# Softmax denominators: ones-products on TensorE against 32x32 transposes and sums on VectorE

## Chip, cores and metric

The kernel runs on one core of one Trainium2 chip, in float32 throughout. The metric is the device time of one execution in microseconds (us), as the median of repeated runs. The engines are TensorE (PE in the profile; its weight loads are listed apart as PEld), VectorE (DVE), ScalarE (ACT), GpSimd (POOL) and the queue that issues the transfers (SP).

## What is computed

Attention over 8 sequences, 12 heads, 448 tokens and 64 values a head, with q and k normalised by their root mean square, followed by a gated feed-forward block of width 1536 on the 3584 rows of 768. Cut to what matters here:

```
q_n, k_n = rmsnorm(q, g_q), rmsnorm(k, g_k)
scores = q_n @ k_n.T / sqrt(64)
attn = exp(scores - max)
attn = attn / (sum(attn, axis=-1) + 1e-9)     # the denominators
x = attn @ v                                  # then (B,H,S,D) -> (B*S, H*D)
xn = x / rms(x) * rms_g
out = (silu(xn @ w_gate) * (xn @ w_val)) @ w_out
```

## The kernel before

The function that runs is `safe_scores`; a second function, `any_scores`, follows only where a flag computed from g_q and g_k asks for it, which it does not for these inputs. The exponentials are taken without the maximum, which a bound on the scores allows.

**Pairs and blocks.** Work goes by pairs of heads: 48 pairs g, six to a sequence (NPAIR = 6). Scores lie transposed, keys on partitions and the 448 queries along the columns, so that a denominator is a sum over partitions. From pair 7 on, a block of the program does seven times: scores of pair g for 64 keys of both heads (`scores`, L659), the weighted values of pair g-1 (`weighted`, L674), and the exponentials (`exps`, ScalarE, L664) into a tile e. These matmuls use quarters of the array (64 by 64). After the block come feed-forward steps (`todo`, run by `fill`), and the turning of the next pair's q and k (`turn`).

**The order.** It is written out by hand: each engine gets its instructions in the order in which the program issues them. The program counts steps: every call of `pe(fn)` is one step, which runs `fn` and then whatever `after(n, ...)` has put down for that step. A block takes four steps for its scores and values, then about 9 to 17 for the rest. In the first sequence's feed-forward steps the weights are also converted (`convert`, with `join` on VectorE, L917 to L919), one piece after most steps. For the second and third sequences VectorE also makes combinations of weights (L1091, L1094, L1126, L1154 to L1157).

**The denominators.** `later_sums(g, 2)`, called at the end of the block's four steps, has GpSimd add the seven tiles e of pair g into a tile es (L709, L714) over the next steps: the first add two steps later, the last ones three steps after that. In es, 64 partitions belong to each head. `totals(g)` runs for g = 7 alone, and then for two pairs at a time, (8, 9), (10, 11) up to (46, 47), in the first step of the block after the second pair, ahead of that block's scores. For each pair and head a matmul with a 64x64 matrix of ones (L692) gives the sum over the 64 partitions, repeated on 64 rows, in a bank `den` of the pool `ps_s` (four banks, shared with the scores). ScalarE copies den into a tile rd (L696, and L699 in two halves). `invert` (L595 to L599) then has VectorE transpose rd in 32x32 blocks, take the reciprocal of one column of each block (14 columns), and transpose these columns, broadcast, back into rd. `weigh` (L638) multiplies the values by rd: for the older pair at once, from a copy in SBUF that `hold` made; for the newer in the block's last step, from PSUM.

Each float32 matmul stands in the trace as two passes, so its rows count double.

Of the kernel before, what the change touches and what calls it, by code (L numbers as in the profile page):

```python
# [22 lines left out]
NPAIR = H // 2  # L23
# [312 lines left out]
def safe_scores(  # L336
# [62 lines left out]
    def own(j):  # L399
        return slice(j * D, (j + 1) * D)  # L400

    def across(j):
        return own(1 - j)
# [189 lines left out]
    def invert(rd, den):  # L593

        few = tmp.tile([128, S // 32], F32, name="few", tag="few", bufs=1)  # L595
        squares_of = lambda t: t.rearrange("p (n c) -> p n c", c=32)
        nc.vector.transpose(out=squares_of(rd), in_=squares_of(den))
        nc.vector.reciprocal(few, squares_of(rd)[:, :, 0])
        nc.vector.transpose(out=squares_of(rd), in_=few.unsqueeze(2).to_broadcast([128, S // 32, 32]))  # L599
# [22 lines left out]
    def close(g):  # L622
        for key in [key for key in st if key[0] == "e" and key[1] == g]:
            st.pop(key)
        for key in ("qk", "v", "qT", "kT", "rs", "ms"):
            st.pop((key, g))

    def hold(g):

        nc.scalar.copy(x_of(g), st.pop(("av", g))[:, 0:S])  # L630
        close(g)
# [45 lines left out]
    def step(g, i):  # L677
# [3 lines left out]
        if ps is not None:  # L681
            exps(g, i, ps)

    def totals(g):

        which = (g, g - 1) if g > NPAIR + 1 else (g,)
        den = {i: ps_s.tile([128, 512], F32, name="den", tag="s") for i in which[::-1]}
        for i in which:
            es = st.pop(("es", i))
            for j in range(2):  # L690
                to = j if i == g else 1 - j
                nc.tensor.matmul(den[i][own(to), 0:S], lhsT=ones[across(j)], rhs=es[across(j)], start=True, stop=True)  # L692
        for i in which[::-1]:
            rd = st["rd", i] = tmp.tile([128, S], F32, name="rd", tag="rd", bufs=2)
            if i == g:
                nc.scalar.copy(rd, den[i][:, 0:S])  # L696
            else:
                for j in range(2):
                    nc.scalar.copy(rd[own(j)], den[i][across(j), 0:S])  # L699
        for i in which[::-1]:  # L700
            invert(st["rd", i], st["rd", i])
            if i < g:
                weigh(i, 3, 4)

    def later_sums(g, n):

        def first():
            st["es", g] = tmp.tile([128, S], F32, name="es", tag="es", bufs=2)
            nc.gpsimd.tensor_tensor(st["es", g], st["e", g, 0], st["e", g, 1], ALU.add)  # L709
            more(2)  # L710

        def more(*parts):
            for i in parts:
                nc.gpsimd.tensor_tensor(st["es", g], st["es", g], st["e", g, i], ALU.add)  # L714

        after(n, first)
        after(n + 2, lambda: more(3, 4))
        after(n + 3, lambda: more(5, 6))


    def rms_x(b):
# [1022 lines left out]
    load_v(1)  # L1744
    gqk = const.tile([128, 1], F32, name="gqk")
    rg = const.tile([128, NDC], F32, name="rg")
    row = const.tile([1, 2, D], F32, name="row")

    def gains():


        nc.vector.scalar_tensor_tensor(gqk, gq, D**0.5, gk, ALU.mult, ALU.mult)
        nc.vector.tensor_scalar(gqk, gqk, SAFE, -SAFE, ALU.min, ALU.max)
# [51 lines left out]
    for g in range(NG + 1):  # L1805
        b, hp = divmod(g, NPAIR)
        if g:
            load_pair(g + 3)
        if hp == 2:
            for i in range(2):  # L1810
                load_rests(b + 1, i, nc.sync)
            load_v_rests(b + 1)
        if g == 0:
            pe(lambda: score(0, (0,)))
            pe(lambda: rests(0))
            pe(lambda: score(0, (1,)))
            pe(lambda: turn(1, 0))
            pe(lambda: score(0, (2,)))
            norm_rests(0, 2, 4)
            squares(2, 0)  # L1820
            squares(2, 1)
            pe(lambda: turn(1, 1))
            for _ in range(3):
                convert()
            load_pair(3)
            load_v(2)
            convert()
            load_rows()
            continue
        if g <= NPAIR:  # L1830
            pe(lambda: score(g, (0,)))
            squares(g + 2, 0)
            squares(g + 2, 1)
            if g > 1:
                pe(lambda: turn(g + 1, 0))
                some_rests(g)
                pe(lambda: turn(g + 1, 1))
            pe(lambda: rests(g))
            pe(lambda: values(g - 1))
            if g == 1:  # L1840
                pe(lambda: turn(g + 1, 0))
                some_rests(g)
                pe(lambda: turn(g + 1, 1))
            load_v(g + 2)

            turns(1 if g == 1 else 3 if g < NPAIR else 0)
            pe(lambda: sums(g - 1))
            pe(lambda: score(g, (1, 2)))
            turns(2 if g == 1 else 3 if g == NPAIR else 0)
            if g == 2:  # L1850
                bound()
            if g == NPAIR - 1:
                for half in range(2):
                    norm_k(g + 2, half)
            continue

        if g == NPAIR + 1:
            some = lambda *parts: [exps(g, i, scores(g, i)) for i in parts]
            pe(lambda: (rests(g), some(0, 1)))
            pe(lambda: values(g - 1))  # L1860
            pe(lambda: rms_x(0))
            pe(lambda: some(2, 3))
            pe(lambda: some(4, 5))
            pe(lambda: norm_x(0))
            pe(lambda: sums(g - 1))
            later_sums(g, 2)
            begin(0, 15)
        else:
            sums_due = g % 2 == 0
            pe(lambda: (totals(g - 1) if sums_due else None, step(g, 0)))  # L1870
            if st.pop("held", None):
                convert()
            pe(lambda: [step(g, i) for i in (1, 2)])
            pe(lambda: [step(g, i) for i in (3, 4)])
            pe(lambda: ([step(g, i) for i in (5, 6)], weigh(g - 1, 2) if sums_due else hold(g - 1)))
            if g < NG:
                later_sums(g, 2)
        st["block"] = now["t"]
        after(2, lambda g=g: load_v(g + 2))
        if hp:  # L1880
            fill()
            norm_k(g + 1, 0)
            squares(g + 2, 0)
            squares(g + 2, 1)
            pe(lambda: turn(g + 1, 0))
            norm_k(g + 1, 1)
            some_rests(g)
            fill()
            pe(lambda: turn(g + 1, 1))
            fill(hold=g % 2 == 1)  # L1890
            continue
        fill(3)
        norm_k(g + 1, 0)
        fill(2)
        pe(lambda: turn(g + 1, 0))
        norm_k(g + 1, 1)
        fill(1)
        pe(lambda: rms_x(b - 1))
        squares(g + 2, 0)
        squares(g + 2, 1)  # L1900
        pe(lambda: turn(g + 1, 1))
        fill(len(todo))
        begin(b - 1, 16)
        pe(lambda: norm_x(b - 1))
        fill()
# [41 lines left out]
```

## Time and profile before

| what | value |
|---|---|
| median of 3 runs | 1515.41 us (1513.07 to 1515.65) |
| profiled execution, span | 1514.0 us |
| PE busy | 1478.8 us (98%) |
| PEld busy | 1154.0 us (76%) |
| DVE busy | 1037.7 us (69%) |
| ACT busy | 602.2 us (40%) |
| POOL busy | 741.3 us (49%) |
| products of the denominators (L692) | 164 rows, 113.2 to 1292.0 us |

The page gives the profiled execution by its span, from the first instruction to the last; what lies around the span is not in it. A share of busy time is a mean over stretches that differ: the first 110 us are attention alone, to about 250 us the weights are converted beside the first feed-forward block, and the rest repeats by sequences. In a timeline row stand the start, the length, engine, line, operation, written tile and read tiles, shapes and count; in brackets the idle time before it and what ended it. In a row of groups stand the count, then busy time, mean ns of one, and the idle time before them.

### The profile page before, as it was taken

The page shows a single profiled execution, that of the slowest core. Times are in us where ns is not written, and L with a number is a line of the kernel's source. Part 1 is how long each engine was busy: PE and PEld are TensorE (multiplying, and loading weights), DVE is VectorE, ACT ScalarE, POOL GpSimd, SP SyncE. Part 2 cuts the span into 40 slices and gives each one's busy share as a digit, 9 for nine tenths or more (in the row PEclk, how much of TensorE's full clock was granted, in tenths as well). Part 3 has the DMA queues.
Part 4 walks back from the last instruction along what each step waited for, and adds up shares of the span by engine and source line. Part 5 has one row for each costly group of instructions (what it writes and reads, how often), then busy time and mean ns, then how long its engine had stood idle before and what let it go on. Part 6 is the DMA issues. An engine that isn't in the chain of part 4 may idle for free.

```text
span 1514.0 us, 25709 instructions
## 1 busy us (share of the span) xinstructions
PE 1478.8 (98%) x8732; PEld 1154.0 (76%) x8732; DVE 1037.7 (69%) x1826; ACT 602.2 (40%) x1377; POOL 741.3 (49%) x708
## 2 busy tenths in 40 slices
PE   8999999999899999999999999999999999999997
PEld 4344445678755888878888888768888789899997
DVE  5788999699944697874568555535668655684664
ACT  6856764344323433234343443443542433101100
POOL 6867997556423454564535643445645731021002
PEclk9999999999999999999999999999999999999999
DMA  7758675776667899996558855585558655587675
GB/s 200 227 159 252 174 247 174 228 249 206 224 219 224 266 316 312 301 291 180 163 150 257 244 176 153 165 255 159 153 153 255 216 162 139 165 292 234 174 228 180
DMA packets 302176, 322.51 MB, mean 213 GB/s; under 512 B 81620, under 2 KB 243668, under 8 KB 302036
## 3 DMA queue, kind: packets, MB, share of 16 engines
q1 hardware_dynamic: 301108, 320.58, 69.4%
q8 instruction: 72, 1.18, 0.3%
q14 instruction: 68, 0.56, 0.1%
q10 hardware_dynamic: 800, 0.20, 0.1%
q0 software_dynamic: 128, 0.00, 0.0%
HBM read 266.90 MB, written 53.77 MB: 212 GB/s over the span
## 4 chain that ended last, share of the span: by engine, by line
PE 84%; DVE 8%; DMA 3%; issue 1%; SPq 1%; POOL 1%; ACT 0%; DVEq 0%; POOLq 0%
PE ff L1191 37%; PE ff L1532 13%; PE sc L659 7%; PE av L674 7%; PE ff L1604 6%; PE ff L1461 5%; PE tr L545 2%; PE den L692 1%; PE den L607 1%; PE sc L563 1%; PE av L590 1%; PE ff L1334 1%; DVE l L1406 1%; DMA w<-kept 1%; DVE w L1091 1%
## 5 line engine op out<-in xcount | busy, mean ns | idle before, releaser
L1191 PE MATMUL ff<-x,w 128*128 128x224 f32 x1296 | 259.6, 353 | 1.4 <-DVE pb L1212 1.1
L714 POOL TENSOR_TENSOR es<-es,e 128x448 f32<-128x448 f32 x205 | 253.4, 1236 | 13.6
L1191 PEld LDWEIGHTS ff<-x,w 128*128 128x128 f32 x1296 | 242.7, 190 | 5.4 <-DVE pb L1212 1.4
L659 PE MATMUL sc<-qT,kT 64*64 64x448 f32 x1176 | 231.0, 539 | 0.7 <-DVE x L744 0.7
L674 PE MATMUL av<-e,vt 64*64 64x448 f32 x984 | 193.1, 538 | 0.0
L664 ACT ACTIVATE e<-sc 128x448 f32<-128x448 f32 x294 | 154.2, 547 | 72.6 <-PE sc L659 57.1
L1191 PE MATMUL ff<-xs,w 128*128 128x224 f32 x832 | 165.0, 353 | 2.9 <-issue 1.6
L1191 PEld LDWEIGHTS ff<-xs,w 128*128 128x128 f32 x832 | 155.7, 190 | 6.2 <-issue 3.0
L644 POOL TENSOR_TENSOR ss<-ss,rd 128x448 f32<-128x448 f32 x40 | 47.1, 1178 | 207.2 <-ACT rd L643 206.5
L709 POOL TENSOR_TENSOR es<-e 128x448 f32<-128x448 f32 x41 | 49.2, 1200 | 192.3 <-ACT e L664 192.3
L659 PEld LDWEIGHTS sc<-qT,kT 64*64 64x64 f32 x1176 | 79.2, 133 | 82.1 <-issue 60.1
L1532 PE MATMUL ff<-w,l 128*128 128x192 f32 x630 | 117.8, 328 | 3.7 <-DVE pa L1567 1.7
L515 POOL TENSOR_TENSOR rs<-ms,mhalf 128x12 f32<-128x12 f32 (+1 forms) x50 | 115.9, 2319 | 4.2
L1212 DVE TENSOR_TENSOR pc<-ff,l 128x448 f32<-128x448 f32 x56 | 34.8, 622 | 115.7 <-PE ff L1191 80.9
L1604 PE MATMUL ff<-x,w 128*128 128x448 f32 x288 | 111.8, 541 | 0.0
L1532 PEld LDWEIGHTS ff<-w,l 128*128 128x128 f32 x630 | 103.8, 190 | 8.7 <-DVE pa L1567 2.9
L674 PEld LDWEIGHTS av<-e,vt 64*64 64x64 f32 x984 | 66.0, 133 | 41.6 <-issue 41.6
L1604 PEld LDWEIGHTS ff<-x,w 128*128 128x128 f32 x288 | 53.3, 190 | 51.1 <-issue 48.2
L1191 PE MATMUL ff<-top_x,w 128*128 128x224 f32 x440 | 91.1, 356 | 0.0
L1209 DVE TENSOR_TENSOR pb<-ff,pb 128x448 f32<-128x448 f32 x84 | 52.3, 623 | 56.1 <-PE ff L1191 50.3
L1191 PEld LDWEIGHTS ff<-top_x,w 128*128 128x128 f32 x440 | 81.8, 190 | 11.3 <-issue 8.5
L1191 PE MATMUL ff<-l,w 128*128 128x224 f32 x416 | 83.6, 353 | 1.1 <-DVE pc L1212 1.1
(212 smaller groups left out, 2806.1 us busy)
## 6 DMA issues: line engine op xcount, KB each, us to landing
w<-kept SPq DMA_DIRECT2D x380, 256.0 KB, 3.5
w<-kept_q SPq DMA_DIRECT2D x350, 192.0 KB, 3.8
w<-kept_o SPq DMA_DIRECT2D x150, 192.0 KB, 3.6
kept_q<-w SPq DMA_DIRECT2D x63, 192.0 KB, 3.9
qk<-in_q_dram SPq DMA_DIRECT2D x48, 192.0 KB, 3.7
qk<-in_k_dram SPq DMA_DIRECT2D x96, 96.0 KB, 3.7
raw<-in_moe_w_gate_dram SPq DMA_DIRECT2D x24, 384.0 KB, 4.8
raw<-in_moe_w_val_dram SPq DMA_DIRECT2D x24, 384.0 KB, 4.4
```

The costliest lines, as they stand in the source:

```text
L515: nc.gpsimd.tensor_tensor(st["rs", g][:, cols], ms, mhalf[:, cols], ALU.pow)
L644: after(m, lambda: (nc.gpsimd.tensor_tensor(ss, ss, rd, ALU.add), st.update({("summed", b): hp})))
L659: nc.tensor.matmul(ps[r, 0:S], lhsT=st["kT", g][r, keys_of(i)], rhs=st["qT", g][r, :], start=True, stop=True)
L664: nc.scalar.activation(e, ps[:, 0:S], ACT.Exp)
L674: nc.tensor.matmul(st["av", g][own(j), 0:S], lhsT=vt, rhs=st["e", g, i][r], start=i == 0, stop=i == PARTS - 1, skip_group_check=True)
L709: nc.gpsimd.tensor_tensor(st["es", g], st["e", g, 0], st["e", g, 1], ALU.add)
L714: nc.gpsimd.tensor_tensor(st["es", g], st["es", g], st["e", g, i], ALU.add)
L1191: nc.tensor.matmul(bank[:, w * HT:(w + 1) * HT], lhsT=data(key)[:, (2 * w + c) * 128:(2 * w + c + 1) * 128], rhs=a[left][:, c, :], start=o ...
L1209: nc.vector.tensor_tensor(T[name], ps[:, 0:S], T[name], ALU.add)
L1461: nc.tensor.matmul(ps, lhsT=left_o(b, which, LEFT_O[name], c), rhs=data(("wo", b, name, c)), start=first and c == 0, stop=c == NFP - 1, sk ...
L1532: nc.tensor.matmul(ps, lhsT=a[:, j, :], rhs=data(key)[:, n % 2 * HW:(n % 2 + 1) * HW], start=start and j == 0, stop=j == KG - 1, skip_grou ...
L1604: nc.tensor.matmul(bank[w][:, 0:S], lhsT=data(key)[:, c * 128:(c + 1) * 128], rhs=st["x", 0][:, 3 * half + c, :], start=half == c == 0, st ...
```

## The change

The sum over partitions is split. A new function `fold(g)` has VectorE transpose es in 32x32 blocks in place and sum each block's rows to one column: 14 columns for a pair, in which each of the four quarters of 32 partitions holds its own part of the sums. It is put down for eight steps after the first add of es, or is run by `totals` itself if that comes first. `totals` then has one matmul with a constant 128x128 matrix `other` of zeros and ones, which adds the two quarters of each head, for both pairs together (28 columns). VectorE takes the reciprocal of the 28 columns from PSUM, and transposes 14 of them, broadcast, into each pair's rd. The ones-products, ScalarE's copies into rd and `invert`'s first transposes go from `totals` (`invert` stays for the first pairs, in `sums`). The matrix `other` is made once, by four sums over parts of the identity matrix, at pair 2. The tile `row` of the flag's computation moves from a pool of constants to a buffer of the output tiles' pool.

```
+    def fold(g):
+        es = blocks(st.pop(("es", g)))
+        nc.vector.transpose(out=es, in_=es)
+        if "few_d" not in st:
+            st["few_d"] = tmp.tile([128, 2, S // 32], F32, name="few_d", tag="few_d", bufs=1)
+        nc.vector.tensor_reduce(out=st["few_d"][:, g % 2], in_=es, axis=AX_X, op=ALU.add)

     def totals(g):
-        which = (g, g - 1) if g > NPAIR + 1 else (g,)
-        den = {i: ps_s.tile([128, 512], F32, name="den", tag="s") for i in which[::-1]}
+        which = (g - 1, g) if g > NPAIR + 1 else (g,)
         for i in which:
-            es = st.pop(("es", i))
-            for j in range(2):
-                to = j if i == g else 1 - j
-                nc.tensor.matmul(den[i][own(to), 0:S], lhsT=ones[across(j)], rhs=es[across(j)], start=True, stop=True)
-        for i in which[::-1]:
+            if ("es", i) in st:
+                fold(i)
+        few, n = st.pop("few_d"), len(which)
+        den = ps_s.tile([128, 512], F32, name="den", tag="s")[:, 0:n * S // 32]
+        nc.tensor.matmul(den, lhsT=other, rhs=few[:, 2 - n:].rearrange("p i n -> p (i n)"), start=True, stop=True)
+        few = tmp.tile([128, 2, S // 32], F32, name="few_r", tag="few_r", bufs=1)[:, 2 - n:]
+        nc.vector.reciprocal(few.rearrange("p i n -> p (i n)"), den)
+        for at, i in enumerate(which):
             rd = st["rd", i] = tmp.tile([128, S], F32, name="rd", tag="rd", bufs=2)
-            if i == g:
-                nc.scalar.copy(rd, den[i][:, 0:S])
-            else:
-                for j in range(2):
-                    nc.scalar.copy(rd[own(j)], den[i][across(j), 0:S])
-        for i in which[::-1]:
-            invert(st["rd", i], st["rd", i])
+            nc.vector.transpose(out=blocks(rd), in_=few[:, at].unsqueeze(2).to_broadcast([128, S // 32, 32]))
             if i < g:
                 weigh(i, 3, 4)
...
         after(n + 3, lambda: more(5, 6))
+        after(n + 8, lambda: fold(g) if ("es", g) in st else None)
...
-    row = const.tile([1, 2, D], F32, name="row")
+    row = y_pool.tile([1, 2, D], F32, name="y", tag="y")
+    other = const.tile([128, 128], F32, name="other")
+    def one_per_quarter():
+        for j in range(2):
+            for n in range(2):
+                cols = slice(j * D + n * 32, j * D + n * 32 + 32)
+                nc.vector.tensor_reduce(out=other[:, cols], in_=ident[:, across(j)].rearrange("p (n c) -> p c n", c=32),
+                                        axis=AX_X, op=ALU.add)
...
             if g == 2:
                 bound()
+                one_per_quarter()
```

More of the change, by code (lines that the diff above doesn't have):

```diff
@@ L626, in close, with blocks @@
             st.pop((key, g))
+    def blocks(t):
+        return t.rearrange("p (n c) -> p n c", c=32)
     def hold(g):
```

## The prediction

> **What bounds the kernel now.** I read the page first (span, busy shares, the forty slices, the chain that ended last), then busy times by stage, then the timelines around the denominators.
>
> ```profile
> span 1514.0 us, 25709 instructions
> ...
> PE 1478.8 (98%) x8732; PEld 1154.0 (76%) x8732; DVE 1037.7 (69%) x1826; ACT 602.2 (40%) x1377; POOL 741.3 (49%) x708
> ...
> DVE  5788999699944697874568555535668655684664
> ...
> PE 84%; DVE 8%; DMA 3%; issue 1%; SPq 1%; POOL 1%; ACT 0%; DVEq 0%; POOLq 0%
> ```
>
> TensorE (PE) carries 84% of the chain, VectorE (DVE) 8%. But DVE's digits are 9 in slices 4 to 11 (37.9 us each), so the share of 69% hides a stretch where DVE is full:
>
> ```profile
> 113.00:208.00 95.00, 95.00 (x449) 45.29 (x452) 84.34 (x125) 63.97 (x151) 84.10 (x77) 1.00 0.75 218
> 208.00:250.00 42.00, 41.31 (x195) 20.84 (x199) 40.93 (x63) 24.86 (x57) 34.01 (x31) 1.00 0.71 210
> 290.00:330.00 40.00, 37.85 (x229) 33.02 (x227) 38.30 (x60) 13.69 (x31) 20.33 (x20) 1.00 0.74 242
> 386.00:416.00 30.00, 26.41 (x171) 20.38 (x168) 27.95 (x45) 11.75 (x27) 15.44 (x13) 1.00 0.59 190
> 416.00:457.00 41.00, 38.57 (x157) 21.20 (x157) 17.05 (x37) 9.51 (x23) 10.75 (x10) 0.96 0.72 224
> 457.00:1290.00 833.00, 826.41 (x5261) 690.29 (x5261) 531.56 (x943) 328.52 (x761) 403.04 (x379) 1.00 0.70 213
> ```
>
> The columns are the stretch, its length, busy time of PE, weight load, DVE, ACT, POOL, then clock and DMA. To 208 us PE never rests and DVE is 89% busy; to 250 DVE is 97% busy; at 290 to 330 and 386 to 416 DVE is over 93% busy while PE loses 2.2 and 3.6 us; after 457 PE loses 6.6 us in 833 and DVE is 64% busy. So the change must be priced in three stretches.
>
> **What the old denominators cost PE.** Every second pair's block carries the products; the other is the same block without them.
>
> ```profile
> 860.08 0.59 PE L659 MATMUL sc<-qT,kT 64*64 64x448 f32 x2
> 865.50 0.84 PE L1191 MATMUL ff<-top_x,w 128*128 128x224 f32 x3
> 889.17 0.98 PE L692 MATMUL den<-es,ones 64*64 64x448 f32 x8
> 895.34 0.83 PE L1191 MATMUL ff<-top_x,w 128*128 128x224 f32 x3
> 401.65 0.86 PE L726 MATMUL msx<-ones,ss 128*112 128x1 f32 x8
> 402.37 0.53 PE L545 MATMUL tr<-ident,qk 128*128 128x128 f32 x3
> L1191 PE MATMUL ff<-x,w 128*128 128x224 f32 x1296 | 259.6, 353 | 1.4 <-DVE pb L1212 1.1 <-DVE pc L1212 0.3
> ```
>
> From the block's first row to the next feed-forward row: 5.42 us without, 6.17 with; a set costs 0.75 (the products, and score banks that wait for ScalarE's copies). The new product is one matmul, two passes. The nearest rows are the 8 passes of L726: 402.37 - 401.65 = 0.72, so 0.09 a pass, bound by the weights; 28 columns at L1191's rate (259.6 / 1296 = 0.20 for 224) are 0.025 and hide under it. I take 0.2. Were the passes not to overlap, it would be about L1191's 0.353 twice, 0.7. So a set saves 0.55 where PE is the bound and the operands are ready (0.05 to 0.57). There are 21 sets: pair 7 alone, then (8, 9) to (46, 47).
>
> **What DVE gets.**
>
> ```profile
> L599 DVE STREAM_TRANSPOSE rd<-few 128x448 f32<-128x448 f32 x48 | 31.0, 645 | 1.6
> L597 DVE STREAM_TRANSPOSE rd<-rd 128x448 f32<-128x448 f32 x41 | 26.2, 639 | 55.1 <-ACT rd L699 54.8
> L598 DVE RECIPROCAL few<-rd 128x14 f32<-128x14 f32 x48 | 11.6, 243 | 1.6
> L496 DVE TENSOR_REDUCE ms<-sq 128x6 f32<-128x384 f32 x96 | 48.4, 543 | 29.3 <-ACT sq L493 29.3
> L638 DVE TENSOR_TENSOR x<-x,rd 128x448 f32<-128x448 f32 x20 | 17.9, 893 | 0.7
> L638 DVE TENSOR_TENSOR x<-av,rd 128x448 f32<-128x448 f32 x28 | 17.5, 624 | 6.1 <-PE sc L659 3.6 <-PE av L674 1.5
> ```
>
> A fold is a transpose (0.64) and a reduce of 448 columns (0.543 x 448/384 = 0.63): 1.27 us, 41 times. At a set of two, DVE loses two first transposes and one reciprocal (2 x 0.64 + 0.24 = 1.52) and keeps a reciprocal, two broadcasts and the weighing. Net +1.0 us a set, some 21 us of DVE in all, and its place moves: half lies in the pair's own block, eight program steps after its sum begins. The fold's price could be higher: L638 takes 0.893 with both inputs in SBUF and 0.624 with one in PSUM; at that ratio a fold would be 1.8. The transposes of SBUF tiles show no such rise (0.639 against 0.645), so I keep 1.27. The Trainium skill's GPSIMD Engine Reference, section of specifications, says that GpSimd shares SBUF interfaces with VectorE and collides with instructions in a 2-port mode or with two SBUF inputs; by it a fold stays at 1.27, and were it to count as such an input, the eight folds on the path below would add about 4 us. L638's two rows agree with it.
>
> ScalarE loses its copies of den; it is 40% busy and not on the chain, so beyond the wait inside the 0.75 I count nothing (if that cover went, 0.5 us of copy a set would still be a gain). The four reduces that build the matrix come once, at pair 2, while PE carries the chain: 0, or at most 4 x 0.543 = 2.2 if uncovered. The moved row buffer and the sum's earlier release cost nothing: no DMA is added.
>
> **Where the fold comes too late: pairs 7, 9, 11.** Counting program steps, the fold of the pair that closes a set lies one step before the set for pairs 7, 9 and 11, in the set itself for 13, and 3 to 9 steps ahead from 15 on. The product heads PE's queue for that step, the scores stand behind it, and DVE takes its queue in order and lags:
>
> ```profile
> 113.17 0.59 PE L692 MATMUL den<-es,ones 64*64 64x448 f32 x2
> 114.86 0.61 DVE L1615 SCALAR_TENSOR_TENSOR h<-h,ff 128x448 f32<-128x448 f32 x1
> 119.44 0.62 DVE L638 TENSOR_TENSOR x<-av,rd 128x448 f32<-128x448 f32 x1 [1.23 <-PE av L674]
> 160.51 0.61 PE L692 MATMUL den<-es,ones 64*64 64x448 f32 x4
> 161.21 0.56 DVE L919 SCALAR_TENSOR_TENSOR top<-raw,top 128x384 int32<-128x384 int32 x1
> 207.88 0.61 PE L692 MATMUL den<-es,ones 64*64 64x448 f32 x4
> 210.59 1.26 DVE L919 SCALAR_TENSOR_TENSOR top<-raw,top 128x384 int32<-128x384 int32 x1
> 249.67 0.59 PE L659 MATMUL sc<-qT,kT 64*64 64x448 f32 x2 [0.69 <-DVE x L744]
> 274.50 0.65 DVE L597 STREAM_TRANSPOSE rd<-rd 128x448 f32<-128x448 f32 x1 [7.95 <-ACT rd L699]
> ```
>
> The DVE rows at 114.86, 161.21 and 210.59 are the last before the fold's place. Pair 7: fold from 115.47 to 116.74 against a product that started at 113.17, 3.6 late, less the 0.55 saved: +3.0. Pair 9: 161.77 to 163.04 against 160.51: 2.5 - 0.55 = +2.0. Pair 11: 211.85 to 213.12 against 207.88: 5.2 - 0.55 = +4.7. DVE's idle row at 119.44, ended by PE, shows that PE's lateness is handed on rather than made good. Of the third, PE wins back the wait at 249.67 (0.69 and the step it breaks, about 0.8), so +3.9. At 274.50 DVE stands idle until PE's products come, so PE's lateness goes on into the rest. Together **+9.0** (4.3 if only the first two carry over, 10.6 if nothing is won back). GpSimd has finished these sums before DVE reaches them, so DVE's lag is the later of the two. Pair 13's fold lies in the set's own step but meets the idle DVE of the last row: between 0 and 1.27, of which I take 0.3, since only the end of GpSimd's sum is in front of it.
>
> **Where DVE is full: 290 to 416.**
>
> ```profile
> 330.23 0.98 PE L692 MATMUL den<-es,ones 64*64 64x448 f32 x8
> 334.16 0.64 DVE L597 STREAM_TRANSPOSE rd<-rd 128x448 f32<-128x448 f32 x1
> 385.86 0.61 PE L692 MATMUL den<-es,ones 64*64 64x448 f32 x4
> 388.29 0.64 DVE L597 STREAM_TRANSPOSE rd<-rd 128x448 f32<-128x448 f32 x1
> ```
>
> The new den holds one of the four score banks until DVE's reciprocal has read it, where ScalarE's copy freed it. The fourth score after it needs that bank some 2.5 us after the product (0.25 and three steps of 0.75). DVE reaches that place at 334.16, 3.9 behind: with 0.24 for the reciprocal, at least 1.7 of waiting at pair 15 and next to none at 17 (2.4 behind). With the folds of 14 to 17 carried along (1.27 each, less what gaps absorb), 15 would wait 3.9 and 17 2.0, and the fold of 18 would add 1.27. Bounds 1.7 and 7.2; I take **+4**, nearer the middle because DVE meets PE in between.
>
> **The rest.** Fifteen sets (19 to 47) save 0.55 each, and 13 saves 0.55 - 0.3: **-8.5**. Of the later folds, that of pair 24 falls at about 604 where DVE works without a gap: 1.27. Those of 25, 26, 31, 32, 43, 44 fall beside the output products that use DVE's fresh operands: 0 to 1.27 each, 0.2 taken, as DVE is 64% busy there. **+2.5** (0 to 8.9).
>
> Sum: 9.0 + 4 - 8.5 + 2.5 = +7.0. It is made against the profiled execution, whose span is 1514.0: 1521.0 for its span. The median of the runs is 1515.41, 1.4 more, and I carry that over: **1522.4**, put down as 1522.
>
> **The rivals.** (1) DVE, not PE, sets 113 to 284, so that the three early waits vanish into waits that were coming anyway. For it: DVE 97% busy to 250. Against: PE has no idle time to give up there but 0.7. 1522.4 - 9.0 = 1513.4, no change.
> (2) Faster: DVE reaches each fold 1.3 us or more before PE reaches the product, at every set; that is the point where it decides. Then 21 x 0.55 = 11.6 is saved: 1503.9. For it: DVE waited in 15 of 20 sets. Against: the three lags above. The Trainium skill's Perfetto Trace Analysis, Identifying the Most-Contended Engine, says to relieve the fullest engine first; that is PE here, and by that rule this rival would be the forecast.
> (3) The long waits lower PE's clock. The trace has one such place:
>
> ```profile
> 418.43 2.19 PE L1461 MATMUL ff<-w,top 128*128 128x384 f32 x4 [3.63 <-DMA w<-kept_o]
> ```
>
> After that wait the stretch 416 to 457 shows a clock of 0.96, so 0.04 x 41 = 1.6 us lost. The waits of 3.6 and 5.2 us, and 3.9 at pair 15, could do the same: 1522.4 + 1.6 for one or 4.9 for three, about 1525. The Trainium skill's TensorE: Matmul & The Clock Gate, What's actually happening, says that an idle window of about 3.4 us halves the clock; the row agrees.
> (4) The small product is no cheaper than what it replaces (0.7 as bounded above, or more): the 8.5 goes, 1530.9.
>
> **Chances.** Forecast 0.50 (alone 1516 to 1527), (1) 0.16, (2) 0.11, (3) 0.17, (4) 0.06. The range 1512 to 1528 leaves out (2) and (4), 0.17. About 0.2%, 3 us, is what can be told from no change: slower is (3), (4) and nine tenths of the forecast, 0.69; same (1) and the forecast's low end, 0.20; faster 0.11.
>
> **What would show it.** PE idle ahead of den at pairs 7, 9 and 11 of 3.6, 2.5 and 5.2 us, released by DVE's reduce; den's idle near zero from pair 19 on, and blocks of 5.6 instead of 6.17; a score at pair 15 released by the reciprocal; a reduce row near 0.63. Wrong if den waits nowhere, or if PE gains idle of the same size less elsewhere before 284.

## The result and the profile after

The changed kernel takes 1533.24 us (median of 5 runs, 1530.44 to 1535.37), the kernel before 1515.41 (5 runs, 1513.07 to 1518.69): a ratio of 1.0116 [1.0097, 1.0136], slower by 1.2%. The forecast was 1522, with a range of 1512 to 1528: the direction was right, the loss was more than twice as large. The profiled execution of after is the shortest of its five (1530.44); its span is 14.6 us longer than that of before, and the working below is made against these 14.6.

First the page of after: span, engines, and the shares of the chain that ended last.

```profile
span 1528.7 us, 25346 instructions
...
PE 1476.6 (97%) x8610; PEld 1159.5 (76%) x8610; DVE 1049.0 (69%) x1851; ACT 576.1 (38%) x1316; POOL 739.6 (48%) x708
...
PE 71%; DVE 18%; issue 3%; DMA 3%; POOL 2%; ACT 1%; SPq 1%; DVEq 0%; POOLq 0%; ACTq 0%
```

PE has 2.2 us less to do and DVE 11.3 more; neither explains 14.6. The chain does: DVE's share went from 8% to 18%. Next the stretches (columns as in the prediction).

```profile
113.00:208.00 95.00, 89.05 (x413) 42.39 (x413) 78.36 (x116) 58.57 (x138) 75.33 (x71) 0.96 0.70 204
208.00:250.00 42.00, 37.11 (x147) 18.12 (x146) 34.34 (x50) 20.57 (x48) 30.80 (x27) 0.92 0.62 184
```

From 113 to 250, PE was busy 136.3 of 137 us before and is busy 126.2 now, and its clock fell from 1.00 to 0.96 and 0.92. Two things were lost there: PE waits, and PE then runs slowly. The timelines of PE and DVE of after show the waits:

```profile
114.77 0.61 DVE L1623 SCALAR_TENSOR_TENSOR h<-h,ff 128x448 f32<-128x448 f32 x1
115.30 0.63 DVE L690 STREAM_TRANSPOSE es<-es 128x448 f32<-128x448 f32 x1
115.96 0.62 DVE L693 TENSOR_REDUCE few_d<-es 128x14 f32<-128x448 f32 x1
116.64 0.39 PE L703 MATMUL den<-few_d,other 128*128 128x14 f32 x2 [3.48 <-DVE few_d L693]
167.80 0.40 PE L703 MATMUL den<-few_d,other 128*128 128x28 f32 x2 [2.47 <-DVE few_d L693]
221.39 0.63 PE L703 MATMUL den<-few_d,other 128*128 128x28 f32 x2 [4.89 <-DVE few_d L693]
```

And stretches of 3.4 us around them show the clock:

```profile
114.60:118.00 3.40, 1.36 (x14) 0.81 (x18) 2.85 (x7) 0.02 (x1) 2.07 (x2) 1.00 1.12 359
118.00:121.40 3.40, 3.40 (x24) 1.22 (x20) 1.15 (x3) 2.39 (x5) 1.95 (x2) 0.50 0.84 187
165.80:169.20 3.40, 1.40 (x14) 0.81 (x18) 3.30 (x7) 0.05 (x1) 3.23 (x4) 1.00 0.93 288
169.20:172.60 3.40, 3.40 (x24) 1.27 (x20) 3.30 (x6) 2.35 (x5) 2.87 (x3) 0.50 1.02 288
217.00:220.40 3.40, 0.00 (x0) 0.00 (x0) 3.33 (x5) 0.08 (x1) 3.40 (x4) 1.00 0.29 39
220.40:227.20 6.80, 5.81 (x30) 2.30 (x34) 4.75 (x10) 2.43 (x5) 2.53 (x3) 0.50 0.98 305
```

Each stretch in which PE was idle for 2.0 us or more is followed by one at half clock: 3.4 us after pairs 7 and 9, 6.8 after pair 11, 13.6 in all.

To place the rest I compare where each block of pair g begins in the two traces (the start of the first weight load for its scores), as lateness against before:

| block | before, us | after, late by | what lies in between (after) |
|---|---|---|---|
| 7 | 82.2 | -0.1 | |
| 9 | 136.1 | 4.75 | wait at pair 7 and its half clock |
| 11 | 183.4 | 8.55 | wait at pair 9 and its half clock |
| 14 | 272.8 | 15.9 | wait at pair 11 and its half clock |
| 19 | 425.5 | 18.1 | the stretch where DVE is full |
| 27 | 678.3 | 18.2 | sets of 19 to 25, their folds |
| 47 | 1263.6 | 15.2 | sets of 27 to 45, their folds |
| end | 1514.0 | 14.6 | |

### The profile page after: what moved, and what is told of

It reads as the page before. It is cut to its first block, busy times and chain, and to the rows that moved or that the text cites. A ratio compares the mean times of both kernels' runs of the same rounds, so it can differ in the third digit from the quotient of the medians.

```text
span 1528.7 us, 25346 instructions
## 1 busy us (share of the span) xinstructions
PE 1476.6 (97%) x8610; PEld 1159.5 (76%) x8610; DVE 1049.0 (69%) x1851; ACT 576.1 (38%) x1316; POOL 739.6 (48%) x708
## 4 chain that ended last, share of the span: by engine, by line
PE 71%; DVE 18%; issue 3%; DMA 3%; POOL 2%; ACT 1%; SPq 1%; DVEq 0%; POOLq 0%; ACTq 0%
PE ff L1199 35%; PE sc L662 12%; PE ff L1540 10%; PE ff L1469 5%; DVE l L1414 2%; DVE top L927 1%; PE tr L545 1%; PE ff L1612 1%; PE sc L563 1%; DVE top L926 1%; PE av L590 1%; POOL w L976 1%; DVE ms L496 1%; PE den L607 1%; DVE top L925 1%
## 5 line engine op out<-in xcount | busy, mean ns | idle before, releaser
L721 POOL TENSOR_TENSOR es<-es,e 128x448 f32<-128x448 f32 x205 | 253.1, 1235 | 13.6
L662 PE MATMUL sc<-qT,kT 64*64 64x448 f32 x1176 | 238.2, 552 | 0.6 <-DVE x L752 0.6
L667 ACT ACTIVATE e<-sc 128x448 f32<-128x448 f32 x294 | 159.1, 543 | 163.3 <-PE sc L662 143.7
L677 PE MATMUL av<-e,vt 64*64 64x448 f32 x984 | 200.3, 554 | 0.0
L1199 PEld LDWEIGHTS ff<-top_x,w 128*128 128x128 f32 x440 | 81.8, 190 | 11.3 <-issue 10.6
L1511 POOL TENSOR_TENSOR y<-y,pa 128x384 f32<-128x384 f32 x10 | 11.3, 1152 | 148.5 <-DMA w<-kept_q 111.6
```

What stands on the lines that cost most here:

```text
L662: nc.tensor.matmul(ps[r, 0:S], lhsT=st["kT", g][r, keys_of(i)], rhs=st["qT", g][r, :], start=True, stop=True)
L667: nc.scalar.activation(e, ps[:, 0:S], ACT.Exp)
L677: nc.tensor.matmul(st["av", g][own(j), 0:S], lhsT=vt, rhs=st["e", g, i][r], start=i == 0, stop=i == PARTS - 1, skip_group_check=True)
L1199: nc.tensor.matmul(bank[:, w * HT:(w + 1) * HT], lhsT=data(key)[:, (2 * w + c) * 128:(2 * w + c + 1) * 128], rhs=a[left][:, c, :], start=o ...
```

## The experiments

Late means the lateness of a block as in this table. Lateness and rows are those of one profiled execution of each kernel; medians are of all its runs. The kernel before took 1514.62 us beside e1 to e4, 1514.87 beside e5 to e8 and 1515.71 beside e9 and e10, and each ratio is against the runs beside it.

**e1: the old way up to pair 13, the new one from 15 on.** This tells what the early sets are worth together.

```
+    LAST_OLD = 13
...
     def totals(g):
+        if g <= LAST_OLD:
+            return totals_old(g)
...
-        after(n + 8, lambda: fold(g) if ("es", g) in st else None)
+        after(n + 8, lambda: fold(g) if ("es", g) in st and g > LAST_OLD else None)
```

> The kernel after, but the sets up to pair 13 go the old way (four ones-products, ScalarE's copies, no fold). Theory: in the kernel after, the product waits at pairs 7, 9 and 11 for a fold that VectorE reaches late (3.5 + 2.5 + 4.9 = 10.8 us), and each wait is followed by 3.4 to 6.8 us at half clock (6 us). Both go, and the rest of the kernel after stays: its blocks from 14 on run 15.6 us late at the start of that stretch and 14.6 late at the end, so I expect a time between the kernel before and 2 us under it, 1513 to 1516 us, no half clock before 300 us. Rival (the loss is VectorE's added load wherever it lies): about half of it stays, 1522 to 1526 us.

Measured: 1516.35 us (1513.28 to 1519.07), ratio 1.0009 [0.9999, 1.0019]. Its trace is 1.45 late at block 7, ahead of the first set (a start-up that differs from one execution to another; after, with the same start, has -0.1), and 1.49 at block 14: the early sets account for all of the lateness that after has there. From 14 to 19 it loses 1.3, and from 19 to 47 it gains only 1.8, where fourteen sets (19 to 45) were to gain 7.7. The median lies just above the 1513 to 1516 expected. So the loss is early, and the later gain is mostly missing too; that is a second question.

**e2: the fold three steps earlier, for pairs up to 13.** If only the waiting for the fold costs, this should remove it.

```
-        after(n + 8, lambda: fold(g) if ("es", g) in st else None)
+        after(n + (8 if g > 13 else 5), lambda: fold(g) if ("es", g) in st else None)
```

> The kernel after, but the folds of pairs 7 to 13 are put down three program steps earlier (five steps after the sum's first add, not eight). VectorE does the same work in the same stretch. Theory (the waits are a matter of place): VectorE reaches the folds of 7 and 9 before TensorE reaches the product, that of 11 at about the same time, so the waits fall from 10.8 us to under 1.5 and the half clock goes: 15 us less than the kernel after, 1516 to 1519 us. Rival (VectorE is full to 250 us, so 1.0 us a set must come out of TensorE wherever the fold lies): the waits appear at another row, 1527 to 1533 us.

Measured: 1518.21 us (1516.22 to 1520.8), ratio 1.0022 [1.0012, 1.0032]. No product waits at 7, 9 and 11 any more, and the clock is not halved there. From its timeline of PE, all rows with idle time ahead between 110 and 222 us:

```profile
118.89 0.59 PE L662 MATMUL sc<-qT,kT 64*64 64x448 f32 x2 [1.25 <-DVE few_r L705]
166.88 0.59 PE L662 MATMUL sc<-qT,kT 64*64 64x448 f32 x2 [1.02 <-DVE few_r L705]
217.21 0.59 PE L662 MATMUL sc<-qT,kT 64*64 64x448 f32 x2 [3.36 <-DVE few_r L705]
```

The waits did not vanish, they moved: a score now waits until VectorE's reciprocal has read den's bank. That is the mechanism which the prediction put at pairs 15 and 17, here in other places, 5.6 us together. Less the savings, e2 goes from 1.84 late at block 7 (start-up) to 4.6 at 14.

**e3: idle products in front of the three that wait.** The waits stay and PE is kept busy through most of them, so that only the clock differs.

```
+        if g in (7, 9, 11):
+            warm({7: 10, 9: 7, 11: 14}[g])
         den = ps_s.tile([128, 512], F32, name="den", tag="s")[:, 0:n * S // 32]
```

> The kernel after, with 10, 7 and 14 idle products of the identity with itself ahead of the product of pairs 7, 9 and 11, so that TensorE works through most of each wait (about 2.4, 1.7 and 3.4 us of 3.5, 2.5 and 4.9). The product starts when it did. Theory (the half clock follows from TensorE's idleness): no half clock at 118, 169 and 220 us, 6 us less than the kernel after, about 1527 us. Rival (the half clock is not what costs, or comes for another reason): same time as the kernel after, 1530 to 1535 us.

Measured: 1524.22 us (1523.22 to 1524.65), ratio 1.0056 [1.0039, 1.0073]. The same stretches of e3, and two of its rows:

```profile
114.60:118.00 3.40, 2.15 (x22) 1.42 (x24) 2.85 (x7) 0.01 (x1) 2.09 (x2) 1.00 1.11 355
118.00:121.40 3.40, 3.40 (x40) 1.38 (x36) 1.17 (x4) 3.19 (x7) 1.93 (x2) 1.00 0.89 197
220.30:227.10 6.80, 6.80 (x49) 3.04 (x42) 4.73 (x9) 6.17 (x15) 2.12 (x2) 1.00 0.94 268
```
```profile
116.65 0.39 PE L705 MATMUL den<-few_d,other 128*128 128x14 f32 x2 [1.25 <-DVE few_d L693]
218.03 0.41 PE L705 MATMUL den<-few_d,other 128*128 128x28 f32 x2 [1.78 <-DVE few_d L693]
```

The product of pair 7 starts at 116.65 as in after (116.64), so nothing was won at the wait itself, and the clock stays at 1.00. The span is 1522.5 against after's 1528.7: 6.2 us is what the half clock cost. By the medians it is 9.0, more than the 6 that were expected. The granted clock over the whole execution was 0.991 in the profiled one of after, 0.988 to 0.990 in its other four, and 0.996 or 0.997 in the four of e3: the half clock is in every execution of after, and the profiled one shows the least of it. e3 is 9.7 late at block 14, where after is 15.9.

**e4: the kernel before, with DVE's load alone.** Two sums over es that nobody reads (1.2 us, a fold's time), at the fold's place; products, copies and `invert` stay as they were. It adds 42.6 us to DVE, where the change adds 11.3, because nothing is taken away in exchange.

```
+        after(n + 8, lambda: spare_fold(g) if ("es", g) in st else None)
+    def spare_fold(g):
+        es = st["es", g].rearrange("p (n c) -> p n c", c=32)
+        few = tmp.tile([128, 2, S // 32], F32, name="few_d", tag="few_d", bufs=1)
+        for i in range(2):
+            nc.vector.tensor_reduce(out=few[:, i], in_=es, axis=AX_X, op=ALU.add)
```

> The kernel before with VectorE's load of the fold alone: two reduces of es (0.62 us each) at the fold's place for every pair, whose result nobody reads; the products, the copies and the rest stay. Theory: before 284 us this costs at most 2 us, since no product waits for it; after 284 us some of the 34 folds lie where TensorE waits for VectorE, as in the kernel after, 5 to 9 us; together 1518 to 1525 us. Rival (load alone explains the whole loss): the old products do not wait for it and still 1530 us or more.

Measured: 1525.06 us (1524.32 to 1525.29), ratio 1.0064 [1.0047, 1.008]; span 1522.5, 8.5 over before. The timeline of PE in e4:

```profile
252.50 0.59 PE L659 MATMUL sc<-qT,kT 64*64 64x448 f32 x2 [2.46 <-DVE x L752]
```

Up to block 12 no block begins late (no product waits for the folds there); in block 13 this wait has grown from 0.69 to 2.46. Late at block 14: 2.8, at 19: 5.4, at 47: 8.7. So a fold on DVE in the pair's own block is not free: beyond block 19, where DVE is 64% busy, the load alone costs 3.3 us, of which 1.2 come between blocks 24 and 25, where the trace has a stretch at half clock (612.9 us).

**e5: product and division at the block's end.** Both folds run in the set's first step, and the product, the reciprocal and the two broadcasts in the last step of that block, after all its scores; the weighing of both pairs follows them. Neither the wait for a fold nor the held bank should then be left.

```
     def totals(g):
-        which = (g - 1, g) if g > NPAIR + 1 else (g,)
-        for i in which:
+        for i in set_of(g):
             if ("es", i) in st:
                 fold(i)
+    def divide(g):
+        which = set_of(g)
...
-        after(n + 8, lambda: fold(g) if ("es", g) in st else None)
...
-            pe(lambda: ([step(g, i) for i in (5, 6)], weigh(g - 1, 2) if sums_due else hold(g - 1)))
+            pe(lambda: ([step(g, i) for i in (5, 6)], (divide(g - 1) if g - 1 > 0 else weigh(g - 1, 2)) if sums_due else hold(g - 1)))
```

> The new sums, placed otherwise: both pairs' folds stand in VectorE's queue where the old first transposes stood (the set's first step), and the product, the reciprocal and the broadcasts come in the block's last step, after the scores, for all 21 sets. Theory (place, not work, is what costs): VectorE was idle ahead of the set in 15 of 20 sets of the kernel before, the scores no longer stand behind the product and no score bank waits for the reciprocal, so each set saves the 0.6 us that it saved in the kernel after from pair 27 on; 21 x 0.6 = 13, less 2 to 4 where VectorE is full (290 to 416 us): 1504 to 1508 us. Rival (the added 21 us of VectorE cost wherever they lie, as in the run with the load alone, 8.5): 1510 to 1514 us.

Measured: 1511.42 us (1509.21 to 1513.89), ratio 0.9976 [0.9964, 0.9988]: faster than before, though short of the 1504 to 1508 expected and inside the 1510 to 1514 of its rival. Group and rows of e5:

```profile
L709 PE MATMUL den<-few_d,other 128*128 128x28 f32 (+1 forms) x42 | 8.5, 282 | 1.1 <-DVE few_d L693 1.1
```
```profile
213.08 0.59 PE L662 MATMUL sc<-qT,kT 64*64 64x448 f32 x2 [1.70 <-ACT e L667]
250.77 0.59 PE L662 MATMUL sc<-qT,kT 64*64 64x448 f32 x2 [0.91 <-DVE x L757]
```

All products together wait 1.1 us instead of 11.0. At pairs 7 and 9 the set's half microsecond is won at once (block 11 is 1.07 early), but from 11 to 14 it loses 1.7 with the two waits shown, from 16 to 17 it loses 2.4, and from 24 to 25 another 3.0. From 25 on it gains steadily, from 3.14 late to 2.55 early at 47: 0.52 for each of eleven sets. So the rival's time came, but not by its mechanism: the folds do not cost wherever they lie, the loss lies before block 25.

**e6, e7, e8: the late product from pair 19 on, the old way before; three variants.** e6 is e5 restricted so. In e7 the product comes a step earlier, after the block's third step. In e8 the older pair's fold stays at its place in its own block.

```
     def totals(g):
+        if g <= 18:
+            return totals_old(g)
```
```
-            pe(lambda: [step(g, i) for i in (3, 4)])
+            pe(lambda: ([step(g, i) for i in (3, 4)], divide(g - 1) if sums_due and g - 1 > 18 else None))
```
```
+        after(n + 8, lambda: fold(g) if ("es", g) in st and g > 18 and g % 2 == 0 else None)
```

> As the late product, but the sets up to pair 17 go the old way with no fold, so that VectorE has no added work before 420 us. Theory: 15 sets save 0.6 each, 9 us, nothing is lost before: 1505 to 1507 us. Rival (folds cost wherever they lie; the load alone cost 3.3 us after 420): 1508 to 1511 us.

> As the one before, but the product comes after the block's third step, some 3.9 us into it, so two scores stand behind it. Folds that end later than that make TensorE wait: where VectorE lags by 2.1 us (pairs 25, 31, 43) two folds end 4.6 us in, 0.7 us of wait each; the older pair is weighed sooner. Theory: 1 to 3 us more than with the product in the last step, 1506 to 1510 us. Rival (the order of these two makes no difference): the same within 1 us.

> As the late product from pair 19 on, but the older pair's fold stays where the change put it, eight steps after its sum begins, and only the newer pair's fold lies in the set's step. Theory: the folds of 22, 24, 26, 32 and 44 lie where TensorE waits for VectorE and cost again what they cost in the kernel after (0.4 to 0.95 each, 4 us in all): 1508 to 1511 us. Rival (only the amount at the set's step matters): less work there, 1504 to 1506 us.

| | median, us | ratio to before | late at 19 | at 25 | at 47 |
|---|---|---|---|---|---|
| e6 | 1510.21 (1507.94 to 1514.41) | 0.9966 [0.9955, 0.9977] | 3.36 | 4.94 | -0.77 |
| e7 | 1515.56 (1512.67 to 1516.59) | 1.0006 [0.9996, 1.0015] | -0.11 | 0.11 | -0.55 |
| e8 | 1515.88 (1513.72 to 1520.39) | 1.0008 [0.9996, 1.0019] | 0.78 | 2.73 | 2.02 |

All three missed the times expected; that of e6 is the one its rival gave (1508 to 1511). The trace of e6 is of its slowest execution and begins 2.8 late (block 7), that of e8 1.8 late, so only differences between blocks count. What they tell lies between 25 and 47: e6 gains 5.7 us in eleven sets, e7 0.7 and e8 0.7. In e8 only the older pair's fold stands elsewhere, so that fold's place in its own block costs about 5 of the 5.7: from 620 to 1290 us TensorE waits 3.4 us at L1228 for VectorE's tiles y and pb in e8, and never at the same place (L1227) in e6. In e7 the product waits for a bank in the blocks of 26, 32 and 44, and each of the three costs 0.9 (block 26 begins 0.3 early and ends 0.6 late); that is 2.7 of the 5.0 by which it gains less than e6, and where the rest goes is open. One of the three in its timeline:

```profile
651.85 0.38 PE L732 MATMUL den<-few_d,other 128*128 128x28 f32 x2 [0.66 <-ACT e L667]
```

Between 19 and 25 e6 gains nothing (it is 1.6 later); where that goes I have not isolated.

**e9: e2, with den's bank freed by ScalarE.** A copy of the 28 columns, then the reciprocal from SBUF, to test that the bank is what e2 waits for.

```
-        nc.vector.reciprocal(few.rearrange("p i n -> p (i n)"), den)
+        flat = few.rearrange("p i n -> p (i n)")
+        nc.scalar.copy(flat, den)
+        nc.vector.reciprocal(flat, flat)
```

> The kernel with the folds of 7 to 13 put down three steps earlier, and ScalarE copies the 28 columns of den to SBUF before VectorE takes the reciprocal there, so that the score bank is free after the copy, however far VectorE lags. Theory: with the early folds the waits moved to the score that needs den's bank (1.25, 1.02 and 3.36 us at pairs 7, 9 and 11, ended by the reciprocal); these 5.6 us go to under 1, 1513 to 1516 us against 1518. Rival (VectorE's lag shows at the next thing that TensorE needs from it): the waits turn up elsewhere and the time stays within 2 us of 1518.

Measured: 1517.74 us (1514.12 to 1518.97), ratio 1.0007 [0.9997, 1.0016]. In its timeline the three waits for the bank are gone, and between 110 and 222 us this one is left:

```profile
209.21 0.40 PE L703 MATMUL den<-few_d,other 128*128 128x28 f32 x2 [0.87 <-DVE few_d L693]
```

From block 7 to 14 it falls back 0.7 us (1.63 to 2.29), e2 2.8 (1.84 to 4.61). So the bank is confirmed in the trace. The time is not: the median stayed above the 1513 to 1516 expected and within the rival's 2 us of 1518, and the intervals of the two ratios (1.0007, and 1.0022 for e2) still overlap. In its trace e9 loses 3.1 from block 24 to 25, where its clock is halved.

**e10: each set in the way that its stretch bears.** Late product for pairs 7 and 9 and from 27 on, the old way for 11 to 25, where e5 and e6 lost.

```
     def totals(g):
+        if 11 <= g <= 25:
+            return totals_old(g)
```

> The late product, with the old way for the sets of pairs 11 to 25, where the traces showed VectorE full or late. Theory: sets 7, 9 and 27 to 47 save about 0.55 each, 7 us, and nothing is lost between: 1507 to 1509 us, under the 1510.2 of the late product from 19 on. Rival (what the runs lost between 19 and 27 was chance of the weight loads, not the folds): no better than that one, 1510 to 1512 us.

Measured: 1506.01 us (1505.45 to 1508.53), ratio 0.9939 [0.9925, 0.9953]; the fastest version here. Three of its stretches, and a row of its timeline:

```profile
407.99:411.40 3.41, 1.04 (x5) 1.05 (x6) 3.34 (x8) 1.15 (x2) 3.17 (x3) 1.00 0.92 271
411.40:414.80 3.40, 3.40 (x11) 2.57 (x11) 3.33 (x7) 0.56 (x1) 0.98 (x2) 0.50 0.94 335
416.00:457.00 41.00, 40.10 (x188) 21.62 (x190) 17.53 (x38) 10.81 (x26) 10.77 (x10) 1.00 0.72 225
```
```profile
417.69 1.56 PE L1497 MATMUL ff<-w,top 128*128 128x384 f32 x4 [0.90 <-DMA w<-kept_o]
```

It is 1.1 early at block 11 and has lost this again at 14. From 27 to 47 it goes from 4.4 early to 9.5 early: 5.2 us from ten sets, 0.52 each, which is the change's own gain. The rest is waits for transfers. At about 418 the wait for a transfer is 0.90 instead of 3.63: 2.8 won between blocks 18 and 19. The half clock that follows this wait before (0.96 from 416 to 457) is not gone in e10; it lies at 411.40, behind a wait for VectorE (2.39) that before has too. There it slows work behind which PE waits for that transfer anyway. Another 2.0 come between 23 and 25, where before waits twice:

```profile
578.76 3.26 PE L1191 MATMUL ff<-xs,w 128*128 128x224 f32 x16 [1.30 <-DMA w<-kept]
...
615.16 2.19 PE L1532 MATMUL ff<-w,top 128*128 128x192 f32 x12 [1.25 <-DMA w<-kept_q]
```

In e10 the first of these is gone and the second is 0.91. Why the transfers come earlier there has not been tried. So the time is under the 1507 to 1509 expected by another route: the ten sets bring what they should, those of 7 and 9 lose their gain again by block 14, and 4.7 us come with the shorter waits for transfers, which no expectation had.

## Why the prediction was right or wrong

The 14.6 us of lateness against the prediction's terms (7.0 in sum):

| term | predicted | measured | from |
|---|---|---|---|
| waits at pairs 7, 9, 11, less the saving | +9.0 | +9.7 | e3 at block 14 |
| half clock behind them | 0 (a rival) | +6.2 | after less e3 |
| 284 to 420 | +4 | +2.1 | after, block 14 to 19 (+5.0 to block 18, then -2.8) |
| sets and folds to the end | -6.0 | -3.4 | after, block 19 to end |

The medians differ by 17.8 us, 3.2 more than these spans. The lower clock of the executions of after that were not profiled fits this, but no trace shows it.

**Right: the three waits.** Forecast 3.6, 2.5 and 5.2 us, measured 3.48, 2.47 and 4.89, each ended by DVE's reduce, and the DVE rows at 114.77 to 115.96 follow each other as worked out. It is the DVE queue in order, not GpSimd's sum, that makes the fold late. One part of it was wrong: the 0.8 to be won back at 249.67 was not, as DVE was late there too. The bounds beside it don't follow from its terms either: 3.0 + 2.0 is 5.0 and not 4.3, and with nothing won back they make 9.7, which is what was measured, and not 10.6. In after a wait of 0.57 remains:

```profile
265.43 0.59 PE L662 MATMUL sc<-qT,kT 64*64 64x448 f32 x2 [0.57 <-DVE x L752]
```

**Right: the prices.** Groups and rows of after:

```profile
L690 DVE STREAM_TRANSPOSE es<-es 128x448 f32<-128x448 f32 x41 | 26.0, 634 | 4.6 <-POOL es L721 4.6
L693 DVE TENSOR_REDUCE few_d<-es 128x14 f32<-128x448 f32 x41 | 25.4, 620 | 1.4
L703 PE MATMUL den<-few_d,other 128*128 128x28 f32 (+1 forms) x42 | 7.0, 248 | 11.0 <-DVE few_d L693 10.8
```
```profile
906.99 0.30 PE L703 MATMUL den<-few_d,other 128*128 128x28 f32 x2
912.64 1.59 PE L1199 MATMUL ff<-top_x,w 128*128 128x224 f32 x7
```

A fold is 0.634 + 0.620 = 1.25 us (1.27 forecast). The block with a set is 912.64 - 906.99 = 5.65 (5.6 forecast, 6.17 before). Of den's 11.0 us of waiting, 10.84 is the three waits. Rival 4, the product no cheaper, falls. The added work of DVE was also right: by its groups the change adds some 22 us (21 forecast). That DVE is busy only 11.3 us longer comes from other instructions that took less time, the weighing from SBUF (`x<-x,rd`) alone 4.5 us less; more on this below.

**Wrong: the clock, the main step.** It was put down as a rival with 0.17, priced at 1.6 us for each wait of 3.6 us and more, from the one place where the trace before showed it. It came after all three waits, that of 2.47 us included, and for twice the length after the third. The mistake was to take the length of that one wait for the condition. What counted before was already less than a full stretch of idleness; PE works for 0.67 us of the 3.40 ahead of the half clock:

```profile
415.70:419.10 3.40, 0.67 (x2) 0.35 (x3) 3.37 (x7) 0.00 (x0) 0.00 (x0) 1.00 0.96 305
419.10:422.60 3.50, 3.50 (x7) 1.99 (x7) 3.40 (x8) 0.48 (x1) 0.00 (x0) 0.52 1.03 360
```

The Trainium skill, TensorE: Matmul & The Clock Gate, What's actually happening, gives an idle window of about 3.4 us; here PE was idle for 2.0 us of a stretch of 3.4, and that was enough. Nor is 1.6 us the price of one event: the three together cost 6.2. Adding the half clock as measured to the forecast, 1522.4 + 6.2 = 1528.6, removes over half of the miss.

**Partly wrong: where DVE is full.** The cost was taken as +4 from a bank that den holds at pairs 15 and 17 (3.9 and 2.0). In after PE waits for DVE ahead of that, at the feed-forward banks (the two rows below; 1.08 and 1.07 at their places before), so that at 15 and 17 there was little left:

```profile
316.42 1.78 PE L1199 MATMUL ff<-x,w 128*128 128x224 f32 x8 [2.28 <-DVE pb L1220]
346.84 3.35 PE L1199 MATMUL ff<-l,w 128*128 128x224 f32 x8 [2.57 <-DVE pc L1220]
```

The second of these is followed by another half clock (the row is 3.35 long where 1.78 is usual). The mechanism of the bank was right, as e2 and e9 show, but in other places. That the sum came out at +2.1 is in part luck. Up to block 18 after loses 5.0 us (e3, without that half clock, 3.8), and then 2.8 come back before block 19: there before waits 3.63 for a transfer (418.43), and after, being late, finds it landed. No term of the prediction had this.

**Wrong in size: the later folds.** Set down at +2.5 with bounds of 0 to 8.9. From block 19 to 47 the change gains 18.06 - 15.19 = 2.9 us, where fourteen sets (19 to 45) would bring 7.7 at 0.55, or 8.5 at the 0.61 that two blocks without disturbance gain (17.85 late at block 28, 17.24 at 30): so the folds cost about 5 to 6 us between them. The list of PE's waits from 457 to 1290 us shows them:

```profile
PE ff L1199 <- DVE pb L1217: 2.9, 2, 2.0
PE ff L1199 <- DVE y L1587: 1.7, 3, 0.6
PE ff L1540 <- DVE pc L1575: 1.5, 3, 0.5
```

The same list of before has 0.8 for the first and nothing for the others, so PE waits 5.3 us more for DVE (e4's list has 2.3, nothing and 1.4). e4 (3.3 by the load alone) and e8 (about 5 by the place of one fold in two) agree that they are not hidden. "DVE is 64% busy there" was no cover, because the queue is in order and a fold stands ahead of whatever PE wants next. How it goes at one such place, in DVE's timeline of after:

```profile
688.91 0.64 DVE L690 STREAM_TRANSPOSE es<-es 128x448 f32<-128x448 f32 x1
689.58 0.62 DVE L693 TENSOR_REDUCE few_d<-es 128x14 f32<-128x448 f32 x1
690.12 1.46 DVE L780 TENSOR_TENSOR raw<-x 128x448 f32<-128x448 f32 x1
691.61 1.30 DVE L780 TENSOR_TENSOR x<-x 128x448 f32<-128x448 f32 x1
```

The instruction behind the fold took 1.46. In e4's timeline, where it falls at another moment, it is 0.66:

```profile
679.78 0.66 DVE L780 TENSOR_TENSOR raw<-x 128x448 f32<-128x448 f32 x1
```

The mean of its group rose from 0.807 to 1.109 us:

```profile
L772 DVE TENSOR_TENSOR raw<-x 128x448 f32<-128x448 f32 x7 | 5.6, 807 | 0.0
```
```profile
L780 DVE TENSOR_TENSOR raw<-x 128x448 f32<-128x448 f32 x7 | 7.8, 1109 | 0.0
```

(first before, then after). That is 2.2 us in seven instructions. The traces say when it happens. Both this group and the weighing `x<-x,rd` read two tiles in SBUF; over all twelve traces, 210 of these instructions had no GpSimd instruction running beside them, and each took 0.61 to 0.63 us; 114 had one, and took 0.61 to 1.54. So none was long without a meeting with GpSimd's work. It goes both ways: the weighing, 893 ns in the mean before, meets GpSimd less often in after:

```profile
L641 DVE TENSOR_TENSOR x<-x,rd 128x448 f32<-128x448 f32 x20 | 13.4, 669 | 0.7
```

The prediction had taken the 893 as the price of two inputs in SBUF. It is a mean of two kinds, 0.62 alone and up to 1.53 beside GpSimd. How the 5 to 6 us divide between the place in the queue and such meetings is not settled.

**The rivals.** (1), the waits vanish: wrong, they carried on to the end. (2), faster: wrong for this change. e5 and e10 are faster, once the product is moved to where its fold is ready, which was the point put down as deciding. That e10's 1506.01 comes near the 1503.9 given for it is partly luck, since about half of its gain comes from transfers. By its rule of relieving the fullest engine the Trainium skill's Perfetto Trace Analysis would have chosen that rival. In after PE is relieved by 2.2 us and the kernel is 1.2% slower, since the product's operand came from a queue that was full at that stage; e10 relieves PE too and is faster, so here the place decided. (3) had the right mechanism at too low a price. (4) has the time that lies nearest, 1530.9, by chance: its mechanism did not occur. One reading at the start was also wrong: DVE's digits are not 9 throughout slices 4 to 11, the eighth is a 6; the stretches that the sum used are right.

## What to carry to other kernels

Before moving work from the busiest engine to a less busy one, place the new instruction in the other engine's queue at each stage: the product that needs its result must come later than that queue gets there, and no other instruction that the busy engine awaits should stand behind it. Count a wait of TensorE of two to three microseconds not by its length alone but with the half clock that may follow it, here another 6.2 us for 10.8 of waiting. The same change, put late in the block where the operand is ready and left out where VectorE is full, went from 1.2% slower to 0.6% faster, of which the sets brought a little over half.

## What the runs showed of the hardware

**Half clock after less idle time than expected.** It came in stretches of 3.41 us, or of two, and in each trace all changes of the clock lie whole multiples of 3.41 us apart, except at the very end: a grid of windows, whose start differs from one execution to another. Over all twelve traces of this case, every window in which PE and its weight loads together were idle for 2.0 us or more (of 3.41) was followed by half clock, and none with up to 1.84. In between it came after 1.85 (e3, at 1510.6) and 1.87 (e4, at 609.5) and not after 1.92 (e6). It is the idle time within the window that counts, not the wait: e2's wait of 3.36 us lay across two windows (1.84 and 1.51), and the clock stayed. The same wait of 2.39 us at 410 us was split between two windows before and was followed by nothing; in e10 it lay in one, and half clock followed. The waits at pairs 7 and 9 of after made 2.05 and 2.01 us of idle time, just enough, so their half clock hangs in part on where the grid fell.

**One window or two.** After the wait at pair 11 a second window of half clock followed, and so it did once in e9 (608.5). In these two, PE was still idle for 0.99 and 0.68 us of the first; in the other windows at half clock before the end it was idle for at most 0.39, and the clock came back after one. Two cases don't make a rule, but no trace here contradicts it.

**The tuned kernel has one as well**, behind the wait of 3.63 at 418.43. So has every trace here, between 411 and 432 us, e10's at 411.40.

**Two inputs in SBUF.** A VectorE instruction on two tiles of 128x448 in SBUF took 0.61 to 0.63 us alone and up to 1.54 when a GpSimd instruction ran beside it (the two groups above, twelve traces); the two instructions of a fold, with one input each, stayed at 0.63 to 0.65 and 0.62 in after, though 49 of these 82 ran beside GpSimd too.
